# Values by head groups, row sums as GpSimd additions and six more VectorE steps in a mixed attention kernel

## The chip, the cores and the metric

The kernel runs on one core of a Trainium2 chip. The metric is the device time of one launch in microseconds, as the median of several runs. The core has TensorE (PE in the profile), VectorE (DVE), ScalarE (ACT), GpSimd (POOL) and SyncE (SP), which here only issues DMAs.

## The reference

There is one sequence of 2048 rows with 512 columns, in bf16, and 32 heads of 16 columns.

```python
g = sigmoid((x * gate_w).sum(-1, keepdims=True))
# branch A, linear attention: feature maps of q and k
pq = einsum("bhsd,hdf->bhsf", q, w_phi);  pk likewise from k
phi_q = concat([softmax(pq), softmax(-pq)]);  phi_k likewise
kv = einsum("bhsf,bhsd->bhfd", phi_k, v);  z = phi_k summed over s
a = (phi_q @ kv) / (phi_q @ z + 1e-6)  @ A_wo
# branch B, softmax attention on the same x with its own weights
p = softmax(q @ k.T * 16 ** -0.5);  b = (p @ v) @ B_wo
return g * a + (1 - g) * b
```

## The kernel before

Most of the work is branch B: 32 heads of 2048 x 2048 scores, each of which needs an exponential. The heads are handled in 32 *sets*, one for each of 4 chunks of 512 queries (`qc`), 4 groups of eight heads (`g`) and the two parities of heads in the group (`par`). A set goes over the 16 tiles of 128 keys (`kt`). Each `kt` gives two score tiles of 128 x 1024 in PSUM (`qk`, line 752), and two engines share the exponentials. For most `kt` ScalarE takes the exponential itself (line 771, two instructions). For the others, whose number for each set stands in `NDVE` (117 in all), VectorE builds the exponential from integer operations in a *step*: two reads of scores into 16-bit integers (line 761, `di`), then over 2048 elements a mask (line 777, `dm`), a product (line 780, `dw`) and a second mask (line 784, `de`). TensorE multiplies either result with the values (`pv`, lines 794 and 807); a VectorE step needs two such products of four matmuls, a ScalarE one needs one. The values lie in `vB`, with 16 columns and a column of ones for each head.

Around this stand *fills*: the projections of q, k and v (`q_proj`, `k_proj`, `v_proj`, all through line 475), branch A and the output projection (lines 891 and 899). Values are made two row tiles at a time for all heads at once, in a 1024-wide PSUM tile of the ring `R_r` that the scores use as well, and VectorE evacuates them (line 469, `vB`). All of that falls into the first two sets, whose entries in `NDVE` are 1 and 1.

Branch A makes 32 feature-map tiles (`phi`, 16 for keys and 16 for queries). Each has a fill, two exponentials on ScalarE (line 634) into one of four buffers of 1024 (`eA_r`, in the space of the weights `WAT`), row sums of 16 elements on VectorE (line 636), an addition of the sums into a check value on GpSimd (line 638), a reciprocal on VectorE (line 640) and the product on GpSimd (line 641).

Rows 0 to 511 of x are loaded plainly and turned on TensorE (line 550), with the two halves copied by ScalarE (line 553) and VectorE (line 554). The other three chunks of 512 rows come by transposing DMAs (line 409) on the SP queue.

The order on each engine isn't written by hand: `_Sched` lists the operations with priorities (in units `ut`, 32 to a set), assumed durations and dependencies, places them one after another, and writes the order of each engine with semaphore waits. It keeps GpSimd operations and the VectorE operations `dm`, `dw`, `de` and `qm` apart in its plan (`shared`, `port`); nothing enforces that at run time.

Of the kernel before, what the change touches and what calls it, by code (L numbers as in the profile page):

```python
# [6 lines left out]
BF16 = mybir.dt.bfloat16  # L7
# [3 lines left out]
ALU = mybir.AluOpType  # L11
# [22 lines left out]
VROW = H * VW + 16  # L34
NDVE = [1, 1, 4, 4, 4, 3, 4, 4, 3, 4, 3, 4, 4, 3, 5, 4, 4, 3, 4, 3, 5, 3, 4, 4, 5, 3, 4, 4, 4, 3, 5, 4]
# [11 lines left out]
STAY = 1.0  # L47
PAIRS = (0, 1, 2, 3, 4, 5, 6, 7)
RUSH = 1.5
HOLD = 0.4  # L50
WARM = 10
RUSH_K = 20.0
RUSH_O = 25.0
RUSH_1 = 8.0
QLEAD1 = 28
LATE_A = 0
VLEAD = 3.0
KLEAD1 = 24
KLEAD = 40
QLEAD = 32  # L60
EARLY = 8.0
# [268 lines left out]
def _build(ctx, nc, A_x, A_wqkv, A_w_phi, A_wo, B_wqkv, B_wo, gate_w, out):  # L330
# [19 lines left out]
    vB_ = sb([128, NT, VROW], name="vB")  # L350
    vB = vB_[:, :, 0:H * VW].rearrange("p t (h c) -> p t h c", c=VW)
    vA = sb([128, NT, 8, 66], name="vA")
# [22 lines left out]
    eA_r = _Slots([watv[:, 1024 * i:1024 * (i + 1)] for i in range(4)])  # L375
# [28 lines left out]
    xs = D_all[0].bitcast(BF16).rearrange("p (i c) -> p i c", c=D)  # L404
    op_x0 = dma("sp", -100, 3.6, xs, A_x[0, 0:NQ, :].rearrange("(i p) c -> p i c", p=128), name="x0")
    op_x = [None]
    for c in range(1, QC):
        op_x.append([add("sp", -100 + c, 2.5,
                         lambda e, c=c: e.dma_start_transpose(xT[:, :, NQ * c:NQ * (c + 1)], A_x[0, NQ * c:NQ * (c + 1), :]),  # L409
                         name=f"x{c}", dma=7.0)])  # L410
# [3 lines left out]
    op_wv = dma("act", -98, 6.0, W_Bv[:], wbv[:, :, 2 * D:3 * D], name="wv")  # L414
    op_wk1 = dma("act", -97, 8.0, W_Bk[:, :, 128:D], wbv[:, :, D + 128:2 * D], name="wk")
    op_wq1 = dma("act", -96, 8.0, W_Bq[:, :, 128:D], wbv[:, :, 128:D], name="wq")
    op_wat = add("sp", -90, 3.0, lambda e: e.dma_start_transpose(WAT[:], A_wqkv[:, 0:2 * D]), name="wat", dma=3.0)
# [22 lines left out]
    op_vpad = [pool(-99, 0.2, lambda e: e.memset(vB_[:, :, H * VW:VROW], 0.0), name="vpad")]  # L440
# [59 lines left out]
    def q_proj(g, c, prio, tile, off):  # L500
# [4 lines left out]
        if (g, c) == (0, 0):  # L505
# [3 lines left out]
            for j in range(4):  # L509
                ms.append(add("dve", prio + 0.01 * j, 0.39, lambda e, j=j: e.tensor_scalar(  # L510
                    qt.ap[:, j, :], q3(), masks[:, j:j + 1], None, op0=ALU.mult),
                    deps=[ev, op_masks] + (ms if j == 3 else []), tiles=[qt], name=f"qm{g}{c}{j}"))
            ev_q[g, c] = ms
# [11 lines left out]
    def v_proj(st, n, prio):  # L525

        tile = _Tile(M_r if n == 1 else R_r)
        fs = [fill(prio, tile, 512 * i, lambda t, i=i: xT[:, t, 128 * (st + i):128 * (st + i + 1)], lambda t: W_Bv[:, t, :],
                   op_x[st // 4] + [op_wv], f"vf{st}") for i in range(n)]
        use_wv.extend(fs)  # L530
        src = lambda: tile.ap[:, 0:512 * n].rearrange("p (t h d) -> p t h d", t=n, d=16)
        e1 = evac("dve", prio, lambda: vB[:, st:st + n, :, 0:16], src, fs, [tile], n=512 * n, name=f"vev{st}")
        for i in range(n):
            ev_v[st + i] = e1
# [7 lines left out]
    tx = _Tile(R_r)  # L542
    txv = lambda: tx.ap.bitcast(BF16).rearrange("p (t q) -> p t q", q=NQ)
    xtp = []
    for t in range(KT):

        def fn(e, t=t):
            ins = None
            for i in range(4):
                ins = e.transpose(txv()[:, t, 128 * i:128 * (i + 1)], xs[:, i, 128 * t:128 * (t + 1)], ident[:])  # L550
            return ins
        xtp.append(add("pe", -80 + t, 0.3, fn, deps=[op_x0, op_id], tiles=[tx], mode="full", name="xtp"))
    op_x[0] = [add("act", -80, 0.9, lambda e: e.copy(xT[:, 0:2, 0:NQ], txv()[:, 0:2, :]), deps=xtp[0:2], tiles=[tx], name="xev"),
               add("dve", -80, 0.6, lambda e: e.tensor_copy(xT[:, 2:4, 0:NQ], txv()[:, 2:4, :]), deps=xtp[2:4], tiles=[tx], name="xev")]
    I_r.tenant[0] = _Tile(None)
    I_r.tenant[0].ops = xtp
    tq = _Tile(R_r)
    k_proj(0, 0, -50, tq, 0, "act")
    q_proj(0, 0, -49, tq, 512)
    tk1 = _Tile(R_r)  # L560
# [4 lines left out]
    for st in range(0, NT, 2):  # L565
        if st // 2 in PAIRS:
            v_proj(st, 2, ut(2 * st) - VLEAD)
        else:
            v_proj(st, 1, ut(2 * st) + 0.5)
            v_proj(st + 1, 1, ut(2 * st + 2) + 0.5)  # L570


    for g in range(1, KT):
        base = 64 * g - (KLEAD1 if g == 1 else KLEAD)
        for c in range(QC):
            t = _Tile(M_r)
            k_proj(g, c, ut(base + 8 * c), t, 0)
        t = _Tile(M_r)
# [46 lines left out]
    def phi(prio, w, st, dst, dst_deps, dst_tiles):  # L625

        tile, ee, ss = _Tile(M_r), _Tile(eA_r), _Tile(ss_r)
        f = fill(prio, tile, 0, lambda t: xT[:, t, 128 * st:128 * (st + 1)], lambda t: Wp[:, w, t, :],
                 ev_wp[0] + ev_wp[1] + op_x[st // 4], f"pf{w}{st}")
        if w == 1:  # L630
# [5 lines left out]
        o6 = add("dve", prio + 5, 1.13, lambda e: e.tensor_reduce(  # L636
            ss.ap[:, 0, :], ee.ap.rearrange("p (g f) -> p g f", f=DH), AX.X, ALU.add), deps=o5, tiles=[ee, ss])
# [9 lines left out]
    for st in range(NT):  # L647
        prio = ut(100 + 16 * st)
# [9 lines left out]
    for lo, hi in ((0, 4), (4, 8)):  # L658
        tkv = _Tile(M_r)
        kvo = []  # L660
        for g in range(lo, hi):
# [6 lines left out]
            kvo.append(add("pe", ut(360 + 3 * g), 0.5, fn, deps=op_phk + ev_vA + kvo[-1:], tiles=[tkv], mode="full", name="kv"))  # L668
        kvw = lambda tkv=tkv: tkv.ap[:, 0:260].rearrange("p (g c) -> p g c", c=65)
        op_kz.append(add("dve", ut(384), 0.334, lambda e, kvw=kvw, lo=lo, hi=hi: e.tensor_tensor(  # L670
# [429 lines left out]
```

## Time and profile before

| quantity | value |
|---|---|
| median of 3 runs | 791.6 us (791.0 to 792.72) |
| profiled execution, its own time | 790.62 us |
| its span | 788.8 us |
| mean granted TensorE clock | 0.998 |
| ScalarE busy | 764.3 us, 97% |
| VectorE busy | 710.5 us, 90% |
| TensorE busy | 708.3 us, 90% |
| GpSimd busy | 121.1 us, 15% |

Busy is the time in which an engine had an instruction under way. Matmuls are pipelined and their ends are modelled, so TensorE's busy time includes waiting that overlaps the drain of the matmul in front.

### The profile page before, as it was taken

What the parts mean: (1) busy time and instruction counts of PE and PEld (TensorE: products, weight loads), DVE (VectorE), ACT (ScalarE), POOL (GpSimd) and SP (SyncE); (2) the same over time, 40 slices, a digit from 0 to 9 for tenths busy, and PEclk for the clock granted to TensorE, in tenths of its full rate; (3) what the DMA queues carried; (4) which work ended last, traced back from release to release, by engine and by line L of the source; (5) the groups of instructions that cost most, each with busy time, mean ns of one, the idle gap of its engine ahead of it and who ended that gap; (6) DMA issues with size and microseconds to landing.
All of it is one profiled execution on the core that took longest, in us unless ns stands there. A gap on an engine that the chain in (4) does not pass through costs nothing.

```text
span 788.8 us, 13621 instructions
## 1 busy us (share of the span) xinstructions
PE 708.3 (90%) x5645; PEld 224.7 (28%) x5716; DVE 710.5 (90%) x883; ACT 764.3 (97%) x865; POOL 121.1 (15%) x123
## 2 busy tenths in 40 slices
PE   8899999999999898998888999899998999988886
PEld 3223232222222222332222323222232232222222
DVE  2456999999999999999999999999999999999993
ACT  4989999999999999999999999999999999999995
POOL 7000002022233322111112010310111101120000
PEclk9999999999999999999999999999999999999999
DMA  9100000000000000023110121210111101120000
GB/s 240 28 8 2 11 4 1 10 6 1 14 1 8 9 1 14 1 68 41 28 21 21 30 19 34 48 23 19 27 22 40 35 14 27 35 42 1 7 1 30
DMA packets 55923, 19.57 MB, mean 25 GB/s; under 512 B 48304, under 2 KB 55856, under 8 KB 55856
## 3 DMA queue, kind: packets, MB, share of 16 engines
q1 hardware_dynamic: 52960, 17.06, 10.4%
q10 hardware_dynamic: 2640, 1.57, 0.7%
q8 instruction: 46, 0.75, 0.4%
q14 instruction: 21, 0.17, 0.1%
q0 software_dynamic: 256, 0.02, 0.0%
HBM read 3.69 MB, written 2.10 MB: 7 GB/s over the span
## 4 chain that ended last, share of the span: by engine, by line
ACT 87%; PE 6%; DVE 4%; DMA 2%; SPq 1%; issue 0%
ACT E L771 80%; ACT WAT L634 4%; PE ps L752 2%; ACT phiK L771 2%; PE ps L475 1%; DVE D L761 1%; DMA xT<-in_A_x_dram 1%; ACT vA L771 1%; PE ps L891 1%; PE ps L807 1%; SPq L521 1%; DVE D L777 1%; DVE D L780 1%; SPq L409 1%; PE ps L665 0%; DMA WB<-WB 0%
## 5 line engine op out<-in xcount | busy, mean ns | idle before, releaser
L771 ACT ACTIVATE E<-ps 128x1024 bf16<-128x1024 f32 x766 | 713.2, 1185 | 4.3 <-PE ps L807 2.2
L752 PE MATMUL ps<-q,kT 64*128 64x512 bf16 x2048 | 362.8, 385 | 58.1 <-ACT E L771 45.7
L761 DVE TENSOR_SCALAR D<-ps 128x1024 int16<-128x1024 f32 x234 | 284.5, 1216 | 21.7 <-PE ps L752 21.1
L752 PEld LDWEIGHTS ps<-q,kT 64*128 64x128 bf16 x2048 | 89.8, 93 | 275.2 <-ACT E L771 214.3
L807 PE MATMUL ps<-E,vB 128*32 128x512 bf16 x1532 | 149.1, 389 | 5.0 <-issue 4.3
L780 DVE TENSOR_TENSOR D<-D 128x2048 bf16<-128x2048 bf16 x117 | 141.4, 1209 | 0.6
L794 PE MATMUL ps<-D,vB 128*32 128x512 bf16 x936 | 90.8, 386 | 1.6 <-issue 1.0
L638 POOL TENSOR_TENSOR acc<-acc,ss 128x64 f32<-128x64 f32 x32 | 24.9, 778 | 435.4 <-DVE ss L636 435.4
L777 DVE TENSOR_SCALAR D<-D 128x2048 int16<-128x2048 int16 x117 | 83.8, 717 | 1.1
L784 DVE TENSOR_SCALAR D<-D 128x2048 int16<-128x2048 int16 x117 | 81.7, 698 | 0.1
L807 PEld LDWEIGHTS ps<-E,vB 128*32 128x32 bf16 x1532 | 37.8, 93 | 85.4 <-issue 77.5
L475 PE MATMUL ps<-xT,WB 128*128 128x512 bf16 x111 | 40.2, 388 | 3.3 <-ACT WAT L634 1.4
L634 ACT ACTIVATE WAT<-ps 128x512 bf16<-128x512 f32 x64 | 39.6, 755 | 0.0
L636 DVE TENSOR_REDUCE ss<-WAT 128x64 f32<-128x1024 bf16 x32 | 38.8, 1212 | 0.6 <-ACT WAT L634 0.4
L475 PE MATMUL ps<-Wp,xT 128*128 128x512 bf16 x98 | 38.0, 389 | 0.5 <-DVE OT L469 0.3
L641 POOL TENSOR_TENSOR phiK<-WAT,ss 128x1024 bf16<-128x1024 bf16 x16 | 35.6, 2222 | 10.7 <-DVE ss L640 10.7
L641 POOL TENSOR_TENSOR WB<-WAT,ss 128x1024 bf16<-128x1024 bf16 x16 | 33.5, 2096 | 14.3 <-DVE ss L640 14.3
L794 PEld LDWEIGHTS ps<-D,vB 128*32 128x32 bf16 x936 | 23.7, 94 | 37.5 <-issue 29.0
L469 DVE CAST vB<-ps 128x1024 bf16<-128x1024 f32 x8 | 9.8, 1225 | 22.0 <-PE ps L475 22.0
L835 PE MATMUL ps<-ident,OT 128*128 128x128 f32 x128 | 27.6, 300 | 0.5 <-ACT WAT L634 0.3
L891 PE MATMUL ps<-phiK 128*128 128x512 bf16 x74 | 25.8, 386 | 0.8 <-issue 0.3
L848 POOL TENSOR_TENSOR acc<-acc,rB 128x64 f32<-128x64 f32 x8 | 5.1, 633 | 133.9 <-DVE rB L840 133.9
(98 smaller groups left out, 351.2 us busy)
## 6 DMA issues: line engine op xcount, KB each, us to landing
out_dram<-Wp SPq DMA_DIRECT2D x16, 128.0 KB, 1.7
q<-qs SPq DMA_DIRECT2D x120, 16.0 KB, 1.8
WB<-in_B_wqkv_dram ACTq DMA_DIRECT2D x2, 384.0 KB, 8.6
D<-in_A_x_dram SPq DMA_DIRECT2D x1, 512.0 KB, 4.5
WB<-in_B_wqkv_dram ACTq DMA_DIRECT2D x1, 512.0 KB, 6.8
WAv<-in_A_wqkv_dram SPq DMA_DIRECT2D x1, 512.0 KB, 4.1
phiK<-in_A_wo_dram SPq DMA_DIRECT2D x1, 512.0 KB, 4.0
phiK<-in_B_wo_dram SPq DMA_DIRECT2D x1, 512.0 KB, 4.8
```

Source lines behind the costliest of these rows:

```text
L475: f = add("pe", prio - rush + 0.01 * t, MM, lambda e, t=t: e.matmul(tile.ap[:, off:off + 512], lhsT=lhs(t), rhs=rhs(t), start=(t == 0), st ...
L634: o5 = [add("act", prio + 1, 0.478, lambda e, a=a: e.activation(ev()[:, :, a, :], P(), ACTF.Exp, scale=1.0 - 2.0 * a), deps=[f], tiles=[ti ...
L636: o6 = add("dve", prio + 5, 1.13, lambda e: e.tensor_reduce(ss.ap[:, 0, :], ee.ap.rearrange("p (g f) -> p g f", f=DH), AX.X, ALU.add), dep ...
L641: return add("pool", prio + 7, 1.95, lambda e: e.tensor_tensor(dst().rearrange("p (g f) -> p g f", f=DH), ee.ap.rearrange("p (g f) -> p g ...
L752: ins = e.matmul(r.ap[:, 512 * i:512 * (i + 1)], lhsT=kT[p0:p0 + 64, g, 128 * kt:128 * (kt + 1)], rhs=qt.ap[p0:p0 + 64, 2 * pair + par, :] ...
L761: last_di = [add("dve", when - 6, 1.133, lambda e, r=r, I=I, part=part: e.tensor_scalar(I.ap[:, 1024 * part:1024 * (part + 1)], r.ap, EXP_ ...
L771: exps.append(add("act", when, 0.904, lambda e, r=r, E=E: e.activation(E.ap, r.ap, ACTF.Exp, scale=EXP_SCALE), deps=[q], tiles=[r, E], nam ...
L777: d1 = add("dve", pd, 0.06 + 0.54 * nk, lambda e, I=I, F=F, n=n: e.tensor_scalar(F.ap[:, 0:n], I.ap[:, 0:n], 0x007F, 0x3F00, op0=ALU.bitwi ...
L780: d4 = [add("dve", pd + 0.01 * y, 1.133, lambda e, I=I, F=F, lo=2048 * y: e.tensor_tensor(F.ap[:, lo:lo + 2048].bitcast(BF16), I.ap[:, lo: ...
L784: d2 = add("dve", pd + 0.1, 0.06 + 0.54 * nk, lambda e, I=I, n=n: e.tensor_scalar(I.ap[:, 0:n], I.ap[:, 0:n], -128, 0x0001, op0=ALU.bitwis ...
L794: ins = e.matmul(O.ap[32 * s:32 * s + 32, :], lhsT=vB_[:, kt, VW * h:VW * h + 32], rhs=w.ap.bitcast(BF16)[:, base + 1024 * (s % 2) + 512 * ...
L807: ins = e.matmul(O.ap[32 * s:32 * s + 32, :], lhsT=vB_[:, kt, VW * h:VW * h + 32], rhs=es[s % 2].ap[:, 512 * (s // 2):512 * (s // 2 + 1)], ...
```

## The change

It has four parts, and the order that `_Sched` writes is new throughout, since priorities and constants change with them.

- Values are made by group of eight heads: `v_proj(g, c)` makes four row tiles for one group as 16 matmuls of 128 columns in one 512-wide tile of `M_r`, and VectorE evacuates 512 columns. Only group 0 is due at the start; groups 1 to 3 come with the keys of their group. In `vB` the groups lie in reverse order (`vcol`), and the weights of group 0 are loaded on their own.
- Rows 512 to 1023 of x are loaded plainly as well and turned on TensorE (`turn(1)`).
- The row sums of the feature maps are four GpSimd additions that halve 1024 elements to 64; `eA_r` has two buffers, and one buffer `tr_r` holds partial sums.
- `NDVE` sums to 123 (sets 1 and 2: 3 and 4). The masks of the first q tile are waited for one by one.

```diff
-NDVE = [1, 1, 4, 4, 4, 3, 4, 4, 3, 4, 3, 4, 4, 3, 5, 4, 4, 3, 4, 3, 5, 3, 4, 4, 5, 3, 4, 4, 4, 3, 5, 4]
+NDVE = [3, 4, 4, 4, 3, 3, 4, 4, 4, 4, 4, 4, 4, 3, 3, 5, 5, 3, 4, 4, 4, 3, 5, 4, 4, 3, 4, 4, 5, 3, 5, 3]
...
-STAY = 1.0
-RUSH = 1.5
-HOLD = 0.4
+STAY = 3
+RUSH = 2.0
+HOLD = 0.3
...
-RUSH_O = 25.0
+RUSH_O = 10
...
+PK0 = 170
+PKS = 19
+PQ0 = 480
+PQS = 28
...
-    eA_r = _Slots([watv[:, 1024 * i:1024 * (i + 1)] for i in range(4)])
+    eA_r = _Slots([watv[:, 1024 * i:1024 * (i + 1)] for i in range(2)])
+    tr_r = _Slots([watv[:, 2048:3840].bitcast(F32).rearrange("p (a b) -> p a b", b=64)])
...
+    op_xs = [dma("sp", -100 + c, 4.0 + 4.3 * c, xs[c], A_x[0, NQ * c:NQ * (c + 1), :].rearrange("(i p) c -> p i c", p=128), name="x0")
+             for c in range(2)]
...
-    op_wv = dma("act", -98, 6.0, W_Bv[:], wbv[:, :, 2 * D:3 * D], name="wv")
+    op_wv0 = dma("act", -98, 5.0, W_Bv[:, :, 0:128], wbv[:, :, 2 * D:2 * D + 128], name="wv0")
...
+    op_wv1 = dma("act", -95, 10.0, W_Bv[:, :, 128:D], wbv[:, :, 2 * D + 128:3 * D], name="wv")
...
-    def v_proj(st, n, prio):
-        tile = _Tile(M_r if n == 1 else R_r)
...
+    def v_proj(g, c, prio):
+        tile = _Tile(M_r)
...
+                for t in range(KT):
+                    ins = e.matmul(tile.ap[:, 128 * i:128 * (i + 1)], lhsT=xT[:, t, 128 * (4 * c + i):128 * (4 * c + i + 1)],
+                                   rhs=W_Bv[:, t, 128 * g:128 * (g + 1)], start=(t == 0), stop=(t == KT - 1))
...
-        o6 = add("dve", prio + 5, 1.13, lambda e: e.tensor_reduce(
-            ss.ap[:, 0, :], ee.ap.rearrange("p (g f) -> p g f", f=DH), AX.X, ALU.add), deps=o5, tiles=[ee, ss])
+        o6 = None
+        for n, d in ((8, 1.12), (4, 0.71), (2, 0.5), (1, 0.4)):
+            o6 = add("pool", prio + 5, d, lambda e, n=n: e.tensor_tensor(
+                tr(n), tr(2 * n)[:, :, 0:n], tr(2 * n)[:, :, n:2 * n], ALU.add), deps=[o6] if o6 else o5, tiles=[ee, ss, tr_], name="ared")
...
-        prio = ut(100 + 16 * st)
+        prio = ut(PK0 + PKS * st)
...
-        prio = ut(400 + 32 * st)
+        prio = ut(PQ0 + PQS * st)
```

More of the change, by code (lines that the diff above doesn't have):

```diff
@@ L541, in _build, with turn, fn @@
             deps=[z0], tiles=[tw, tz], mode="full", name="warm")
[L542 to L556, printed above, removed]
+    def turn(c):
+        tx = _Tile(R_r)
+        txv = lambda: tx.ap.bitcast(BF16).rearrange("p (t q) -> p t q", q=NQ)
+        xtp = []
+        for t in range(KT):
+            def fn(e, t=t):
+                ins = None
+                for i in range(4):
+                    ins = e.transpose(txv()[:, t, 128 * i:128 * (i + 1)], xs[c][:, i, 128 * t:128 * (t + 1)], ident[:])
+                return ins
+            xtp.append(add("pe", -80 + t + 33.5 * c, 0.26, fn, deps=[op_xs[c], op_id], tiles=[tx], mode="full", name="xtp"))
+        sl = slice(NQ * c, NQ * (c + 1))
+        op_x[c] = [add("act", -80 + 34 * c, 0.9, lambda e: e.copy(xT[:, 0:2, sl], txv()[:, 0:2, :]), deps=xtp[0:2], tiles=[tx], name="xev"),
+                   add("dve", -80 + 34 * c, 0.6, lambda e: e.tensor_copy(xT[:, 2:4, sl], txv()[:, 2:4, :]), deps=xtp[2:4], tiles=[tx], name="xev")]
+        I_r.tenant[c] = _Tile(None)
+        I_r.tenant[c].ops = xtp
+    turn(0)
     tq = _Tile(R_r)
@@ L564, in _build @@
     k_proj(0, 3, -46, tk2, 0, "act")
[L565 to L570, printed above, removed]
+    for c in range(QC):
+        v_proj(0, c, ut(8 * c) - VLEAD)
     for g in range(1, KT):
@@ L885, in _build @@
         off = 512 if last and i == 1 else 0
-        prio = begin[i] if last else ut(545 + 128 * qc + 6 * i)
+        prio = begin[i] if last else ut(PQ0 + 145 + 4 * PQS * qc + 6 * i)
         sl, sb_ = slice(128 * st, 128 * (st + 1)), slice(128 * i, 128 * (i + 1))
```

90 lines of the change are left out of this document (50 added, 40 removed).

## The prediction

> **What bounds the kernel now.** I read the page's busy times and chain first, then the busy time by stretch, the chain in order of time, the groups by line with shapes apart, and last the timeline of VectorE and GpSimd side by side.
>
> ```profile
> span 788.8 us, 13621 instructions
> PE 708.3 (90%) x5645; PEld 224.7 (28%) x5716; DVE 710.5 (90%) x883; ACT 764.3 (97%) x865; POOL 121.1 (15%) x123
> ACT 87%; PE 6%; DVE 4%; DMA 2%; SPq 1%; issue 0%
> ```
> ScalarE carries the chain and is hardly idle. The time of this execution is 790.62 us, so 1.82 us lie around the span; it is 0.98 us under the median of 791.6. All sums below are against 790.62.
>
> I cut the span at the first exponential, at the end of the first two head sets (60 exponentials on ScalarE) and at its last exponential.
>
> ```profile
> core 0: us, PE busy (x) PEld busy (x) DVE busy (x) ACT busy (x) POOL busy (x), PEclk, DMA share, GB/s
> 0.00:11.55 11.55, 9.17 (x46) 3.89 (x47) 3.24 (x8) 2.89 (x3) 8.08 (x23) 1.00 0.91 243
> 11.55:74.00 62.45, 57.00 (x403) 18.02 (x407) 29.50 (x33) 57.23 (x64) 7.54 (x11) 1.00 0.20 42
> 74.00:777.40 703.40, 636.43 (x5167) 200.29 (x5227) 674.69 (x836) 701.84 (x796) 104.47 (x86) 1.00 0.09 19
> 777.40:788.80 11.40, 5.68 (x43) 2.51 (x36) 3.04 (x8) 2.33 (x4) 1.01 (x3) 0.88 0.17 52
> ```
> After 74 us ScalarE is idle for 703.40 - 701.84 = 1.6 us in all, and VectorE is busy for 95.9%: two full engines, with ScalarE ahead. Before 74 us it is otherwise. ScalarE has 62.45 - 57.23 = 5.2 us of gaps and VectorE is busy for 29.50 of 62.45. That is where the old step counts (1 and 1) leave room.
>
> ```profile
> 1.26 4.49 SPq L409
> 5.81 8.64 DMA xT<-in_A_x_dram
> 43.08 1.19 PE ps L475 x5
> 46.97 1.19 PE ps L475 x5
> 50.16 25.77 ACT E L771 x28
> 133.07 26.58 ACT E L771 x29
> ```
> This is the chain in order of time. Early it runs through the transposing load of x and, at 43 and 47 us, through projections on TensorE; from 50 us it is ScalarE's exponentials back to back, one each 26.58 / 29 = 0.917 us.
>
> **The change part by part.**
>
> *Steps.* The counts go from 117 to 123: sets 1 and 2 from 2 to 7, sets 3 to 32 from 115 to 116. A step moved takes two exponentials off ScalarE: 10 x 0.917 = 9.2 us early and 2 x 0.917 = 1.8 us late. On VectorE a step is two line 761, one 777, one 780 and one 784.
>
> ```profile
> L761 DVE TENSOR_SCALAR D<-ps 128x1024 int16<-128x1024 f32 x234 | 284.5, 1216 | 21.7 <-PE ps L752 21.1
> L780 DVE TENSOR_TENSOR D<-D 128x2048 bf16<-128x2048 bf16 x117 | 141.4, 1209 | 0.6
> L777 DVE TENSOR_SCALAR D<-D 128x2048 int16<-128x2048 int16 x117 | 83.8, 717 | 1.1
> L784 DVE TENSOR_SCALAR D<-D 128x2048 int16<-128x2048 int16 x117 | 81.7, 698 | 0.1
> L636 DVE TENSOR_REDUCE ss<-WAT 128x64 f32<-128x1024 bf16 x32 | 38.8, 1212 | 0.6 <-ACT WAT L634 0.4
> L469 DVE CAST vB<-ps 128x1024 bf16<-128x1024 f32 x8 | 9.8, 1225 | 22.0 <-PE ps L475 22.0
> L469 DVE COPY OT<-ps 128x512 f32<-128x512 f32 x31 | 21.0, 678 | 1.3 <-PE ps L807 1.0
> L641 POOL TENSOR_TENSOR phiK<-WAT,ss 128x1024 bf16<-128x1024 bf16 x16 | 35.6, 2222 | 10.7 <-DVE ss L640 10.7
> L852 POOL TENSOR_TENSOR acc<-acc,rB 128x64 f32<-128x64 f32 x8 | 2.6, 321 | 0.7
> ```
> A step costs (284.5 + 141.4 + 83.8 + 81.7) / 117 = 5.05 us of VectorE; that is a little high, since neighbouring instructions overlap. One more late step is +5.05, five more early ones +25.3.
>
> *Reduce to tree.* The 38.8 us of line 636 leave VectorE, all of them after 74 us. GpSimd gets per tile adds that write 512, 256, 128 and 64 elements. No row has these. Between line 852 (64 elements, 0.32) and the uncontended line 641 below (1024 elements, 1.93, bf16 with one operand broadcast) a straight line gives 0.21 us plus 1.68 ns per element: 1.07 + 0.64 + 0.43 + 0.32 = 2.46 us, 79 us for 32 tiles. GpSimd is busy for 121 us, so it goes to about 200 us, a quarter of the span. The bounds for one tile are 4 x 0.32 = 1.3 us and 4 x 1.93 = 7.7 us; I stay near the line because the ops span it. The Trainium skill, "GPSIMD Engine Reference", section "When to use GPSIMD", gives a reduction along the free dimension to VectorE and calls GpSimd about twice as slow on two-input operations; its 4497 ns for 2048 elements would make the tree about 2.1 us by an estimate, so by the rule as by the rows the sum takes longer on GpSimd than 1.21 us. The sum below is unchanged by it, because the time is taken from an engine with room.
>
> *What the tree costs VectorE.* GpSimd and VectorE hold each other up:
>
> ```profile
> 194.88 2.78 POOL L641 TENSOR_TENSOR phiK<-WAT,ss 128x1024 bf16<-128x1024 bf16 x1 [1.49 <-DVE ss L640]
> 196.93 1.28 DVE L784 TENSOR_SCALAR D<-D 128x2048 int16<-128x2048 int16 x1
> 198.14 0.68 DVE L777 TENSOR_SCALAR D<-D 128x2048 int16<-128x2048 int16 x1
> 229.13 1.93 POOL L641 TENSOR_TENSOR phiK<-WAT,ss 128x1024 bf16<-128x1024 bf16 x1 [0.36 <-DVE ss L640]
> ```
> Line 784 starts at 196.93 while line 641 runs to 194.88 + 2.78 = 197.66, and ends at 198.21, 0.55 us after it: it did nothing until GpSimd was through. How much of this there is now, from the groups for 120 to 700 us, and then for 700 to 777 us, where GpSimd hardly works:
>
> ```profile
> L777 DVE TENSOR_SCALAR D<-D 128x2048 int16<-128x2048 int16 x93 | 67.5, 726 | 0.8
> L784 DVE TENSOR_SCALAR D<-D 128x2048 int16<-128x2048 int16 x92 | 64.7, 703 | 0.0
> L784 DVE TENSOR_SCALAR D<-D 128x2048 int16<-128x2048 int16 x15 | 10.2, 682 | 0.0
> L777 DVE TENSOR_SCALAR D<-D 128x2048 int16<-128x2048 int16 x14 | 9.5, 676 | 0.1
> ```
> 93 x 0.050 + 92 x 0.021 = 6.6 us of stalls for 104.47 us of GpSimd work. The order written by the scheduler mostly keeps the two apart. In that proportion 79 us more cost 5 us; I take 7, since the adds follow ScalarE and not VectorE, so that their start is less tied to VectorE's own order. Were the starts random, 123 x 3 instructions would meet an add with a chance of 79 / 700, 42 times, and wait half of it, length weighted 0.37 us: 16 us. With everything serial it is 79 us. Behind the row stands the Trainium skill, "SBUF — State Buffer", section "SBUF: two separate sides": an exclusive lock on a shared port pair, held for the whole instruction, which also a VectorE operation with two SBUF inputs takes; for line 780 no row here shows that.
>
> VectorE after the first two sets is then 674.69 + 5.05 - 38.8 + 8 x 0.68 (values of two later groups) + 7 = 653.4 us of about 701.6: 93%, less full than now. ScalarE stays the bound there. Its gaps may grow from 1.6 to 2.4 us as stalls bunch: late stretch -1.8 + 0.8 = -1.0 us.
>
> *Slots.* The exponentials of the feature maps get two buffers for four, and one tree buffer. A third tile's exponentials on ScalarE would wait for the first tile's product on GpSimd, and the exponentials of the scores queue behind them.
>
> ```profile
> 123.73 0.98 ACT WAT L634 x2
> ...
> 318.38 0.98 ACT WAT L634 x2
> ```
> The 16 tiles of keys begin on average (318.38 - 123.73) / 15 = 13 us apart, and the new spacing is 19/16 of that, 15.4; the queries' goes from 32 units to 28. The GpSimd chain is 2.46 + 0.32 + 1.93 us and a reciprocal, some 6 us. Zero, then; if the cover went, each tile would hold ScalarE by at most that chain.
>
> *Values by groups.* 64 matmuls of 512 columns become 256 of 128, half of them now after the first two sets.
>
> ```profile
> 5.40 1.05 PE L550 MATMUL ps<-ident,D 128*128 128x128 bf16 x16
> 6.04 1.01 ACT L553 COPY xT<-ps 128x1024 bf16<-128x1024 bf16 x1 [0.54 <-PE ps L550]
> PEld ps L752 <- ACT E L771: 214.3, 600, 0.8
> ```
> At 1.05 / 16 = 0.066 us the early half costs 8.4 us where 64 x 0.238 (1.19 / 5 above) = 15.2 stood: TensorE gets 7 us back in the stretch in which it was the chain. Late it takes 8.4 us, hidden by the 214 us in which it waits for ScalarE. On VectorE 9.8 us of evacuation leave early and 8 x 0.68 = 5.4 come.
>
> *Second load of x.* ScalarE copies one more half block: +1.0 us. The plain load frees the SP queue from one transposition, so rows 1024 onward come sooner; a sixth load on ScalarE's queue lies ahead of the first copy. I count both at zero, with 1 us either way: the first exponential waits for the masks of q, not for either.
>
> *Early sum.* ScalarE's work is 57.23 - 9.2 + 1.0 = 49.0 us. VectorE's is 29.50 - 9.8 + 25.3 + 5.4 + 0.7 (its half of x) = 51.1, some 2 to 3 less with overlaps: both nearly full. So not all gaps vanish; I take 4.0 of the 5.2. The stretch is 53.0 for 62.45: -9.4 us (bounds -13, with no gaps, and -3, with VectorE at 85%).
>
> Sum: 790.62 - 9.4 - 1.0 = 780.2; head and tail unchanged. The median stood 0.98 above the profiled run, which gives 781.2.
>
> **The rivals.** *Forecast* (chance 0.68): ScalarE keeps the chain, 776 to 784.5 us. For it: 1.6 us of gaps in 703 while VectorE was at 95.9%, and VectorE is relieved.
>
> *The early steps don't pay* (0.12): set 1 and 2 become a wait of PV for VectorE. 51.1 us at a fill of 85% are 60 us, so the stretch gains 2 to 3 us for 9.4: 785 to 789.5. For it: before 74 us VectorE waited for TensorE, 22.0 us in front of the value evacuations alone. Against: the projections it waited for are what leaves.
>
> *The lock makes VectorE the bound* (0.16, slower). VectorE today fills 95.9% beside a full ScalarE; of 701.6 us that is 672.8, and without stalls from adds it needs 646.4. So 26.4 us of stalls are free, and each beyond costs about 1.04. The time is over 792.4 from 37.5 us on, nearly half of all adds' time. At 50 us it is 805, with everything serial 836. Against: today 6% of GpSimd's time returns as stalls. The Trainium skill's rule of engine selection, cited above, would favour this rival; the trace so far does not.
>
> *Nothing to be measured* (0.04): gains and stalls cancel, 790 to 793. A difference of 0.2%, 1.6 us, is about the least that a measurement of this kernel can tell.
>
> The likeliest gives 781.2. The range of 775 to 791 holds the forecast and the second case and leaves out the slower case and some of its neighbour. Faster is 0.68 + 0.12 = 0.80, same 0.04, slower 0.16.
>
> **What would show it.** Right: no reduce on VectorE; twelve fewer exponentials in the groups of line 771; the 50th exponential ends near 63 us; ScalarE idle under 3 us from there to its last; an add of 512 at about 1.07 us; lines 777 and 784 at 0.70 to 0.76 on average. Wrong: ScalarE waiting for scores under a VectorE that is above 97% busy, means of 777 and 784 above 0.85, or exponentials of the feature maps waiting for GpSimd.

## The result, and the profile after

The changed kernel takes 787.84 us (median of 6 runs, 786.9 to 789.1) against 791.58 us before. The ratio is 0.9951 with a 95% interval of 0.9937 to 0.9965: faster by 3.7 us, where 10.4 were forecast. The time lies inside the stated range of 775 to 791, but the gain is about a third of the forecast one. The profiled execution took 787.98 us.

The head of the page after, and the busy time in the same four stretches as before: up to the first exponential, to the end of the first two sets (now 50 exponentials), to ScalarE's last exponential, and the tail.

```profile
span 786.2 us, 14251 instructions
PE 731.3 (93%) x5948; PEld 237.2 (30%) x5948; DVE 720.7 (92%) x890; ACT 756.2 (96%) x854; POOL 218.8 (28%) x251
ACT 64%; PE 21%; DVE 12%; issue 1%; SPq 1%; DMA 1%
core 0: us, PE busy (x) PEld busy (x) DVE busy (x) ACT busy (x) POOL busy (x), PEclk, DMA share, GB/s
0.00:14.80 14.80, 11.20 (x67) 5.52 (x68) 3.75 (x9) 3.80 (x5) 8.06 (x23) 0.88 0.99 231
14.80:64.30 49.50, 47.40 (x418) 17.95 (x416) 42.69 (x50) 47.71 (x55) 9.19 (x11) 1.00 0.18 41
64.30:775.50 711.20, 667.28 (x5439) 211.41 (x5435) 671.23 (x825) 702.33 (x794) 200.59 (x214) 1.00 0.09 19
775.50:786.20 10.70, 5.45 (x31) 2.29 (x31) 3.04 (x8) 2.33 (x4) 1.00 (x3) 0.90 0.17 54
```

The first two sets end at 64.3 us for 74.0: the early gain of 9.7 us is there. The third stretch holds two exponentials fewer and yet lasts 711.2 us for 703.4, so 7.8 us of the gain are lost here. ScalarE, which held 87% of the chain, holds 64%, and VectorE and TensorE have come into it, though VectorE is busy for only 671.23 of 711.20 us, 94.4%, less than the 95.9% of before.

The groups of VectorE's product (line 806) and masks (803 and 810), the four GpSimd additions (662) and the feature-map exponentials on ScalarE (656). GpSimd's own product of a feature-map tile is line 667 now and was line 641.

```profile
L806 DVE TENSOR_TENSOR D<-D 128x2048 bf16<-128x2048 bf16 x123 | 150.4, 1224 | 1.0
L803 DVE TENSOR_SCALAR D<-D 128x2048 int16<-128x2048 int16 x123 | 96.6, 786 | 1.2
L810 DVE TENSOR_SCALAR D<-D 128x2048 int16<-128x2048 int16 x123 | 90.0, 732 | 0.2
L662 POOL TENSOR_TENSOR WAT<-WAT 128x512 f32<-128x512 bf16 x32 | 42.0, 1312 | 256.8 <-ACT WAT L656 256.7
L662 POOL TENSOR_TENSOR WAT<-WAT 128x256 f32<-128x256 f32 x32 | 31.4, 981 | 2.4
L662 POOL TENSOR_TENSOR WAT<-WAT 128x128 f32<-128x128 f32 x32 | 19.3, 603 | 2.4
L662 POOL TENSOR_TENSOR ss<-WAT 128x64 f32<-128x64 f32 x32 | 12.4, 388 | 2.5
L656 ACT ACTIVATE WAT<-ps 128x512 bf16<-128x512 f32 x64 | 39.1, 739 | 0.1
```

Lines 803 and 810 were lines 777 and 784 before, at 717 and 698 ns. Summed over the trace after the first two sets, and counting what an instruction took over 0.69 us (masks) or 1.23 us (product) where that is more than 0.1 us, VectorE stalls for 20.0 us in 37 instructions; before it was 6.5 us in 11. By the GpSimd instruction that runs beside them, 11.7 of the 20.0 us lie beside the additions (short ones into check values included), in 29 instructions, and 8.3 us beside GpSimd's product, in 8. Before, all 6.5 us lay beside the product.

One burst shows how a stall reaches ScalarE. It is the timeline of VectorE, then of GpSimd, of TensorE and of ScalarE:

```profile
311.84 0.69 DVE L803 TENSOR_SCALAR D<-D 128x2048 int16<-128x2048 int16 x1
312.44 1.64 DVE L810 TENSOR_SCALAR D<-D 128x2048 int16<-128x2048 int16 x1
314.01 1.75 DVE L806 TENSOR_TENSOR D<-D 128x2048 bf16<-128x2048 bf16 x1
315.68 1.21 DVE L787 TENSOR_SCALAR D<-ps 128x1024 int16<-128x1024 f32 x1
...
311.84 4.17 POOL L662 TENSOR_TENSOR WAT<-WAT 128x512 f32<-128x512 bf16 x3 [4.57 <-ACT WAT L656]
316.09 0.29 POOL L662 TENSOR_TENSOR ss<-WAT 128x64 f32<-128x64 f32 x1
...
316.95 0.60 PE L778 MATMUL ps<-q,kT 64*128 64x512 bf16 x4 [0.74 <-DVE D L787]
...
314.34 2.02 ACT L797 ACTIVATE E<-ps 128x1024 bf16<-128x1024 f32 x2
317.38 1.02 ACT L797 ACTIVATE E<-ps 128x1024 bf16<-128x1024 f32 x1 [1.03 <-PE ps L778]
```

The additions begin when ScalarE's exponentials end, not when VectorE has room. Line 810 takes 1.64 us for 0.69, line 806 right behind it 1.75 for 1.23; line 787, which frees a score tile, starts some 1.5 us late. TensorE waits for it with the next scores (line 778), and ScalarE stands idle for 1.03 us. That VectorE's product, with two inputs in SBUF, is held up as well is what the Trainium skill says in "SBUF — State Buffer", section "SBUF: two separate sides"; the 1.75 us agree.

GpSimd's product does the same, and more:

```profile
257.87 2.25 POOL L667 TENSOR_TENSOR phiK<-WAT,ss 128x1024 bf16<-128x1024 bf16 x1 [2.32 <-DVE ss L666]
258.26 2.41 DVE L803 TENSOR_SCALAR D<-D 128x2048 int16<-128x2048 int16 x1
...
263.58 7.44 ACT L797 ACTIVATE E<-ps 128x1024 bf16<-128x1024 f32 x8 [1.29 <-PE ps L778]
```

It starts 0.39 us ahead of line 803, which then takes 2.41 us for 0.69, and ScalarE pauses for 1.29 us. Of ScalarE's pauses over 0.15 us in the third stretch, five end within 6.5 us of the start of such a stall, 4.7 us in all: three of them (1.29, 0.72 and 0.92 us) behind a stall of 1.72 or 1.73 us beside the product, and two (1.03 and 0.72) behind a burst of 0.95 and 0.52 us beside the additions. No other stall has a pause right behind it but a further 1.0 us in three short ones, while TensorE has half its clock (last section). A pause of 1.41 us at 628 us lies behind the load of a query tile, and two pauses at 94 and 116 us, 0.7 us together, stand in the kernel with short additions and product (below) as well.

### The profile page after: what moved, and what is told of

It reads as the page before. It is cut to its first block, busy times and chain, and to the rows that moved or that the text cites. A ratio compares the mean times of both kernels' runs of the same rounds, so it can differ in the third digit from the quotient of the medians.

```text
span 786.2 us, 14251 instructions
## 1 busy us (share of the span) xinstructions
PE 731.3 (93%) x5948; PEld 237.2 (30%) x5948; DVE 720.7 (92%) x890; ACT 756.2 (96%) x854; POOL 218.8 (28%) x251
## 4 chain that ended last, share of the span: by engine, by line
ACT 64%; PE 21%; DVE 12%; issue 1%; SPq 1%; DMA 1%
ACT E L797 59%; PE ps L778 8%; DVE D L787 4%; PE ps L487 3%; PE ps L833 3%; ACT WAT L656 2%; DVE D L803 2%; DVE D L806 2%; PE ps L917 2%; ACT phiK L797 2%; PE ps L820 2%; DVE D L810 1%; SPq L533 1%; ACT vA L797 1%; PE ps L547 1%
## 5 line engine op out<-in xcount | busy, mean ns | idle before, releaser
L797 ACT ACTIVATE E<-ps 128x1024 bf16<-128x1024 f32 x754 | 703.4, 1144 | 8.7 <-PE ps L778 7.6
L787 DVE TENSOR_SCALAR D<-ps 128x1024 int16<-128x1024 f32 x246 | 298.5, 1213 | 29.4 <-PE ps L778 28.4
L662 POOL TENSOR_TENSOR WAT<-WAT 128x512 f32<-128x512 bf16 (+2 forms) x96 | 92.7, 965 | 261.6 <-ACT WAT L656 256.7
L806 DVE TENSOR_TENSOR D<-D 128x2048 bf16<-128x2048 bf16 x123 | 150.4, 1224 | 1.0
L803 DVE TENSOR_SCALAR D<-D 128x2048 int16<-128x2048 int16 x123 | 96.6, 786 | 1.2
L810 DVE TENSOR_SCALAR D<-D 128x2048 int16<-128x2048 int16 x123 | 90.0, 732 | 0.2
L487 PE MATMUL ps<-xT,WB 128*128 128x512 bf16 x128 | 49.1, 402 | 2.8 <-issue 2.2
L487 PE MATMUL ps<-Wp,xT 128*128 128x512 bf16 x128 | 49.2, 391 | 2.3 <-DVE oB L867 1.8
L917 PE MATMUL ps<-phiK 128*128 128x512 bf16 x88 | 31.4, 387 | 0.6 <-ACT WAT L656 0.6
L487 PE MATMUL ps<-WAv,xT 128*128 128x512 bf16 x64 | 23.5, 388 | 1.7 <-ACT WAT L656 1.6
L481 DVE COPY OT<-ps 128x512 f32<-128x512 f32 x31 | 21.1, 680 | 2.0 <-PE ps L833 1.0
## 6 DMA issues: line engine op xcount, KB each, us to landing
WB<-in_B_wqkv_dram ACTq DMA_DIRECT2D x3, 384.0 KB, 10.3
```

What stands on the lines that cost most here:

```text
L487: f = add("pe", prio - rush + 0.01 * t, MM, lambda e, t=t: e.matmul(tile.ap[:, off:off + 512], lhsT=lhs(t), rhs=rhs(t), start=(t == 0), st ...
L662: o6 = add("pool", prio + 5, d, lambda e, n=n: e.tensor_tensor(tr(n), tr(2 * n)[:, :, 0:n], tr(2 * n)[:, :, n:2 * n], ALU.add), deps=[o6] ...
L787: last_di = [add("dve", when - 6, 1.133, lambda e, r=r, I=I, part=part: e.tensor_scalar(I.ap[:, 1024 * part:1024 * (part + 1)], r.ap, EXP_ ...
L797: exps.append(add("act", when, 0.904, lambda e, r=r, E=E: e.activation(E.ap, r.ap, ACTF.Exp, scale=EXP_SCALE), deps=[q], tiles=[r, E], nam ...
L803: d1 = add("dve", pd, 0.06 + 0.54 * nk, lambda e, I=I, F=F, n=n: e.tensor_scalar(F.ap[:, 0:n], I.ap[:, 0:n], 0x007F, 0x3F00, op0=ALU.bitwi ...
L806: d4 = [add("dve", pd + 0.01 * y, 1.133, lambda e, I=I, F=F, lo=2048 * y: e.tensor_tensor(F.ap[:, lo:lo + 2048].bitcast(BF16), I.ap[:, lo: ...
```

## The experiments

Before was measured anew beside each group of experiments: 791.58 us beside the changed kernel, 792.33 beside the next four kernels, 790.86 beside the four after them and 791.58 beside the last three. Kernels of different groups are therefore best compared by their ratios to before.

**Short additions, and short additions with a short product.** The order of every engine is that of the changed kernel; the additions, then also GpSimd's product, work on 64 elements and leave out the rest.

```diff
-                tr(n), tr(2 * n)[:, :, 0:n], tr(2 * n)[:, :, n:2 * n], ALU.add)
+                row n of tr_ (or ss), 64 elements, from two rows of 64, ALU.add)
...
-            dst()[all 64 groups of 16] = ee * reciprocals
+            dst()[groups 0 to 3] = ee * reciprocals
```

> The changed kernel with the same order on every engine; the four GpSimd additions of a feature-map tile remain, but each works on 64 elements (two of the sixteen terms are summed and doubled three times). Theory (the adds hold the port that VectorE's lines 803, 806 and 810 need, in bursts that reach ScalarE): GpSimd falls by about 65 us, the means of 803 and 810 fall from 0.79 and 0.73 to about 0.72, ScalarE's gaps after the first two sets fall by 4 to 6 us, time 782 to 784 against 788. Rival (the new order and its fill density make the gaps, not the adds): gaps unchanged, 787 to 789.

> As the kernel with short adds, same order, and the GpSimd product of each feature-map tile also works on 64 of its 1024 elements. Theory of the port: the rest of the late gaps that are not a late query load or a clock drop goes too, means of 803 and 810 at 0.68, time 779 to 781. Rival (order): 786 to 789. If the product and not the adds is what hurts, this one gains and the short adds alone do not.

Measured: 784.44 us (ratio to before 0.9892, 0.986 to 0.9925) and 779.88 us (0.9833, 0.9803 to 0.9863). The stretch after the first two sets, and the masks, of the second kernel:

```profile
64.50:767.50 703.00, 647.29 (x5371) 210.81 (x5435) 654.97 (x825) 700.43 (x794) 99.12 (x214) 1.00 0.09 19
L807 DVE TENSOR_SCALAR D<-D 128x2048 int16<-128x2048 int16 x123 | 86.3, 703 | 1.2
L814 DVE TENSOR_SCALAR D<-D 128x2048 int16<-128x2048 int16 x123 | 84.0, 683 | 0.2
```

The order is the same and GpSimd is busy for half as long, with 1.1 us of stalls left: the stretch takes 703.00 us for 711.20, where the forecast had 703.4 - 1.0 = 702.4. One pause of 1.19 us is left in it, in which TensorE waits for a query tile's load. So the new order alone is not at fault. What GpSimd's work does to VectorE costs the changed kernel 787.84 - 779.88 = 8.0 us, or 0.9951 - 0.9833 = 1.2%, 9.3 us, by the ratios: 3.4 us (4.7 by the ratios) with the additions, 4.6 more with the product. The split is rough: with short additions alone the four runs took 783.08 to 787.05 us, and the profile, of the slowest of them, shows gaps of 7.7 us for 8.9, not the 4 to 6 us less that were expected. Its masks have means of 0.744 and 0.694, and its stalls are 9.1 us, of which 8.1 lie beside the product.

**The tree alone.** The kernel before with the four additions, two buffers and the partial-sum buffer, nothing else but the order that `_Sched` then writes.

```diff
-        o6 = add("dve", prio + 5, 1.13, lambda e: e.tensor_reduce(
+        for n, d in ((8, 1.12), (4, 0.71), (2, 0.5), (1, 0.4)):
+            o6 = add("pool", prio + 5, d, ...
```

> The kernel before with one part of the change: the row sums as four GpSimd additions, two buffers for the exponentials and one for partial sums; steps, values, loads and constants as before. My forecast's view (VectorE's relief is worth nothing by itself, stalls stay hidden): 790 to 792, no difference. Theory of the port in bursts: ScalarE's gaps grow by 5 to 8 us, 796 to 799. Rival (order of the rest of the change is to blame): 790 to 792 too, and the loss must then show in the kernel without the tree.

Measured: 799.04 us, ratio 1.0086 (1.0056 to 1.0116). The 38.8 us of the reduction are gone from VectorE, and the kernel is 7 us slower:

```profile
PE 711.8 (89%) x5648; PEld 226.9 (28%) x5716; DVE 695.1 (87%) x851; ACT 766.1 (96%) x865; POOL 223.2 (28%) x251
L782 DVE TENSOR_SCALAR D<-D 128x2048 int16<-128x2048 int16 x117 | 92.9, 796 | 1.1
L785 DVE TENSOR_TENSOR D<-D 128x2048 bf16<-128x2048 bf16 x117 | 145.6, 1245 | 1.0
```

VectorE is at 87%, and the masks of line 782 are at 796 ns for 717; stalls by the same count are 21.3 us, of which 11.5 or a little more lie beside the product and the rest beside the additions. A VectorE with room doesn't protect ScalarE.

**Without the tree.** First the changed kernel with row sums on VectorE, the step counts of before from set 3 on and the feature-map spacing of before.

```diff
-PK0, PKS, PQ0, PQS = 170, 19, 480, 28;  NDVE sums to 123
+PK0, PKS, PQ0, PQS = 100, 16, 400, 32;  NDVE sums to 122
```

> The changed kernel without the tree: row sums on VectorE, four buffers, the step counts of before from set 3 on (3, 4 and then 115, together 122), and the feature-map spacing of before; values by groups and the second plain load stay. Theory (early part works, the loss comes with the tree): early gain of 10 us kept, one less late step costs 1.8, late gaps of 2 to 4 us as VectorE is at 97%: 781 to 784. Rival (VectorE too full without the tree): late gaps of 8 us or more, 787 or slower.

Measured: 808.67 us, ratio 1.0206 (1.0175 to 1.0237). Expected were 781 to 784, and the run tells nothing on the question: ScalarE has three pauses of 12, 6 and 5 us between 157 and 198 us, the longest here, and the scheduler's own order for this kernel holds them.

```profile
151.90 5.89 ACT L792 ACTIVATE E<-ps 128x1024 bf16<-128x1024 f32 x6
169.54 2.10 ACT L792 ACTIVATE E<-ps 128x1024 bf16<-128x1024 f32 x2 [11.74 <-PE ps L773]
```

Then with other spacing and counts (3 and 5, then 114), so that the order has no pause as long as these:

> The changed kernel with the row sums on VectorE again and four buffers; 122 steps (3 and 5 in the first two sets, then 114), keys' feature maps 16 units apart from 170, queries' 32 from 430, chosen so that the order has no long pause of ScalarE of its own, which the earlier kernel without the tree had. Theory (the tree relieves VectorE of about as much as the port takes back): the same as the changed kernel, 786 to 790. Rival A (the tree is a net loss): 780 to 784. Rival B (the tree is worth much, VectorE is too full without it): 794 or more.

Measured: 795.45 us, ratio 1.0051 (1.0028 to 1.0074), with runs from 791.89 to 799.96; the median is in the second rival's reach of 794 or more. The stretch from the 50th exponential on:

```profile
63.50:782.00 718.50, 671.27 (x5413) 211.29 (x5410) 680.62 (x851) 703.18 (x795) 102.83 (x86) 0.99 0.09 19
```

With 3 and 5 steps the first two sets hold 48 exponentials here, which end at 61.6 us; the 50th ends at 63.5, about as early as with the tree. So the early gain needs no tree. But the late stretch is 718.50 us for 711.20. VectorE's work there is 680.62 us, the reduction among it, and ScalarE stands idle for 718.50 - 703.18 = 15.3 us. The kernel is 795.45 - 787.84 = 7.6 us slower than the changed one, with one step fewer in all. That this is the tree's worth is not shown: stalls are 2.6 us here, and of ScalarE's longest pauses only one, of 3.09 us to 72.1 us, has TensorE waiting for VectorE, for a copy; those of 3.59 and 1.79 us, with 1.03 behind, come when TensorE waits for DMAs (2.95 us for a query tile up to 298.4 us, 1.69 us for a turned feature map up to 431.8 us). The order and the spacing of the feature maps differ as well.

**The kernel before with a short product.** If the stalls of before were hidden, taking them away gives nothing.

```diff
-            dst()[all 64 groups of 16] = ee * reciprocals
+            dst()[groups 0 to 3] = ee * reciprocals
```

> The kernel before in its own order, with the GpSimd product of a feature-map tile on 64 of its 1024 elements. My forecast's reading (the 6.6 us of stalls of before are hidden by VectorE's slack): 790 to 792, no gain. Theory (each stall of VectorE reaches ScalarE in part even there): 787 to 789, half the stalls back.

Measured: 790.14 us, ratio 0.999 (0.998 to 0.9999).

```profile
L777 DVE TENSOR_SCALAR D<-D 128x2048 int16<-128x2048 int16 x117 | 79.8, 683 | 1.1
L784 DVE TENSOR_SCALAR D<-D 128x2048 int16<-128x2048 int16 x117 | 78.9, 674 | 0.1
```

The masks are at 0.683 and 0.674 us, about what the prediction took as free (0.676 and 0.682), the stalls are gone, and the kernel gains a tenth of a per cent, 0.8 us. Nearly all of the stalls of before were hidden. What the 6.5 us cost before is 1.6 us at most, by the interval.

**Weights ahead of the second load of x.** Order and work of the changed kernel; two weight loads go from ScalarE's queue to SP's, between the two plain loads of x. This tests the later first exponential of the profile after (14.80 us for 11.55).

```diff
+    for n, o in enumerate((op_wk0, op_wq0)):
+        sch.order["act"].remove(o)
+        o.eng = "sp"
+        sch.order["sp"].insert(1 + n, o)
```

> The changed kernel, every engine's order kept, but the loads of the first weights of keys and queries go out on the SP queue between the two plain loads of x, instead of on ScalarE's queue beside them. Theory (the second plain load delays those weights, and TensorE's clock drops in the wait): first projection near 7.3 us for 8.9, no half clock at 9 us, first exponential at 11.5 to 12.5 for 14.8, time 784 to 786. Rival (start is hidden, since ScalarE waits later for VectorE's steps): 787 to 789.

Measured: 787.61 us, ratio 0.996 (0.9945 to 0.9975): no difference to the changed kernel that could be told (0.2 us less by the medians, 0.7 more by the ratios), as the rival had it. In its profile the first exponential is at 13.74 us, the 50th ends 1.1 us earlier and the last 0.8 us. The start was not what was missing. A single profile's start also proves little: the short-product kernel above loads and starts just as before does and has its first exponential at 15.43 us, not 11.55.

**The product in four pieces.** Everything of the changed kernel is done; the product of 1024 elements is four instructions of 256, so that VectorE could get in between.

```diff
-            dst()[64 groups] = ee * reciprocals
+            for h in range(4):
+                dst()[groups 16h to 16h + 15] = ee * reciprocals
```

> The changed kernel in its order, with GpSimd's product of a feature-map tile in four pieces of 256 elements, one behind the other, semaphore on the last. Theory (VectorE waits for the rest of one GpSimd instruction, so shorter instructions mean shorter waits): means of 803 and 810 fall by 0.03 to 0.05, 784 to 787. Rival (a GpSimd instruction waiting in its queue takes the port again at once, so VectorE waits for all four): unchanged or slower, 788 to 791.

Measured: 786.08 us, ratio 0.9934 (0.9911 to 0.9956).

```profile
L808 DVE TENSOR_SCALAR D<-D 128x2048 int16<-128x2048 int16 x123 | 94.6, 769 | 1.2
L815 DVE TENSOR_SCALAR D<-D 128x2048 int16<-128x2048 int16 x123 | 90.0, 732 | 0.2
```

The masks were at 786 and 732, so little changes; the sum of stalls is 20.5 us for 20.0. But those that last over 0.8 us fall from 7 to 4, ScalarE's pauses right behind stalls fall from 4.7 to 3.0 us, and 1.8 us come back (1.3 by the ratios). That long stalls cost more than the same time in short ones would explain it, but the intervals of the two ratios overlap, so this is weak.

**GpSimd held to the plan.** The scheduler plans times for all operations; on the chip the order on each engine is fixed, but GpSimd starts as soon as its inputs are there. Here each GpSimd operation after 60 us of the plan, the product as well as the additions, also waits for the last VectorE mask or product that the plan starts ahead of it. No work is left out and no order changed.

```diff
+    k, held = 0, [d for d in sch.order["dve"] if d.shared]
+    for o in sch.order["pool"]:
+        while k < len(held) and held[k].start < o.start:
+            k += 1
+        if o.start > 60 and k and o.dma is None:
+            o.deps.append(held[k - 1])
```

> The changed kernel, order of every engine kept and nothing left out; each GpSimd operation after 60 us of the plan also waits for the last of VectorE's mask and product instructions that the plan puts ahead of it. In the changed kernel's trace 20 us of stalls of VectorE lie in 37 instructions, and behind nearly all of them stands a GpSimd operation that the plan has after the VectorE instruction, but that came first because VectorE was later than planned. Theory (it is this overtaking, not the sharing itself, that costs): stalls over 0.1 us fall from 20 to 5 us or less, time 780 to 783. Rival (sharing costs what it costs; a held GpSimd operation only delays the feature maps): 786 to 790.

Measured: 780.81 us, ratio 0.9858 (0.9836 to 0.988).

```profile
64.20:768.50 704.30, 666.10 (x5440) 210.68 (x5436) 662.93 (x825) 700.57 (x793) 163.55 (x214) 1.00 0.09 19
L803 DVE TENSOR_SCALAR D<-D 128x2048 int16<-128x2048 int16 x123 | 86.0, 700 | 1.2
L810 DVE TENSOR_SCALAR D<-D 128x2048 int16<-128x2048 int16 x123 | 89.5, 727 | 0.2
L662 POOL TENSOR_TENSOR WAT<-WAT 128x512 f32<-128x512 bf16 x32 | 37.9, 1184 | 256.9 <-DVE D L806 105.7 <-ACT WAT L656 76.8 <-DVE D L787 38.8
L662 POOL TENSOR_TENSOR WAT<-WAT 128x256 f32<-128x256 f32 x32 | 23.3, 728 | 22.0 <-DVE D L803 11.7 <-DVE D L810 5.9 <-DVE D L806 3.5
L662 POOL TENSOR_TENSOR WAT<-WAT 128x128 f32<-128x128 f32 x32 | 13.3, 415 | 11.2 <-DVE D L803 6.5 <-DVE D L810 1.9 <-DVE D L806 1.2
L662 POOL TENSOR_TENSOR ss<-WAT 128x64 f32<-128x64 f32 x32 | 9.9, 309 | 18.4 <-DVE D L806 12.4 <-DVE D L803 3.3 <-DVE D L810 1.0
```

The additions now wait mostly for VectorE (lines 806, 787, 803 and 810), and the kernel is faster for it, as GpSimd has room. Of the 8.0 us that GpSimd's work took, 7.0 are back (7.4 of 9.3 by the ratios; the interval overlaps with that of the short additions and product). Stalls halve, to 10.3 us in 25 instructions; that is over the 5 expected, and those over 0.8 us fall from 7 to 3. "Nearly all" was said too strongly: of the 26 stalls over 0.2 us in the changed kernel, 16, with 12.9 of 18.5 us, have a GpSimd operation beside them that the plan puts behind the VectorE instruction. Three of the 16 are GpSimd's product, with the stalls of 1.72 and 1.73 us, and all five stalls or bursts with a pause of ScalarE behind them are among the 16. That agrees with about half of the stalls gone. In the held kernel no pause of ScalarE over 0.15 us comes within 8 us behind a stall.

**The same waits on the tree alone.** They hold all of GpSimd's operations, as above.

```diff
+    (the six lines above, in the kernel with the tree alone)
```

> The kernel before with the tree alone, and the same extra waits of GpSimd. Theory (overtaking costs the 7 us of the kernel with the tree alone): 790 to 793, as before, since ScalarE is the bound. Rival: 797 to 800 as without the waits.

Measured: 791.96 us, ratio 1.0002 (0.9987 to 1.0017). The 7 us that the tree cost alone are gone. The order of every engine is that of the kernel with the tree alone.

```profile
74.10:777.00 702.90, 653.69 (x5225) 202.41 (x5225) 649.66 (x804) 701.72 (x796) 167.73 (x214) 1.00 0.09 19
L782 DVE TENSOR_SCALAR D<-D 128x2048 int16<-128x2048 int16 x117 | 82.2, 705 | 1.1
```

VectorE has 649.66 us of work where before had 674.69, and the late stretch is 702.90 for 703.40. ScalarE sets it; relief of VectorE by itself is worth nothing here. Stalls are still 10.8 us, in 21 instructions, and cost nothing that can be told.

**All that helped, together.** The held GpSimd operations, the weights first, and a query load that the plan reckons with 5.0 us for 3.0, because ScalarE has a pause in the changed kernel behind such a load (1.41 us, to 629.5 us). The last edit makes a new plan.

```diff
+    (the six lines above, and the four of the weights)
-    ... name=f"qsp{g}{c}", dma=3.0, parts=8)
+    ... name=f"qsp{g}{c}", dma=5.0, parts=8)
```

> As the changed kernel with the extra waits, and two small repairs: the first weights of keys and queries load on the SP queue between the two plain loads of x, and the load that spreads a query tile is planned at 5 us of latency for 3, so that the order is a new one, with the pause of 1.75 us at 629 us expected to go. Expected 777 to 781; if the pause was luck of the order and another one takes its place, 780 to 783 as with the waits alone.

Measured: 778.35 us, ratio 0.9833 (0.9815 to 0.9852): 13.2 us under before and 9.5 under the changed kernel. The pause behind the query load is gone. Between this and the held kernel lie 2.5 us, which were not divided between the two further edits and the new plan.

```profile
L803 DVE TENSOR_SCALAR D<-D 128x2048 int16<-128x2048 int16 x123 | 85.3, 694 | 1.2
```

## Why the prediction was right or wrong, point by point

**The early part was right.** Forecast was a gain of 9.4 us up to the end of the first two sets; the profiled executions show 74.0 - 64.3 = 9.7. Inside it two things missed in opposite ways: the stretch itself is 49.5 us for the 53.0 of the sum, with VectorE at 42.69 us of work and not some 48 to 51, and ScalarE's work at 47.71 us for 49.0, its gaps at 49.50 - 47.71 = 1.8 us where 4.0 had been left (53.0 - 49.0); against that stood a first exponential 3.25 us later in this profile. So the agreement of 9.4 and 9.7 is partly luck. VectorE's work was less in part because eight more reads of scores and four more products fall into the stretch, four steps and not the five counted. The head was taken as unchanged; part of its 3.25 us is the first projection, which starts at 8.94 us for 7.24 and meets half the clock (0.88 in the first row for 1.00). The second load may be the cause in part: with the weights ahead of it the first exponential came 1.1 us sooner, in one profile.

**The tree's price on GpSimd was nearly right.** A straight line between 64 and 1024 elements gave 2.46 us per tile. With GpSimd held to the plan the four take 1.184 + 0.728 + 0.415 + 0.309 = 2.64. The changed kernel shows 1.312 + 0.981 + 0.603 + 0.388 = 3.28, so VectorE holds GpSimd up as well.

**Slots, tail and the late values cost nothing that shows**, as counted: ScalarE is idle for 0.1 us ahead of the 64 exponentials of line 656, the tail is no longer than before (10.70 us for 11.40), and with short additions and product the late stretch, values in it, is within 0.6 us of the forecast.

**The step that failed is "What the tree costs VectorE"**, and what hung on it, ScalarE's gaps. The sum counted 7 us of new stalls, gaps of 2.4 us and a late stretch shorter by 1.0. Measured were 13.5 us more stalls (6.5 to 20.0), gaps of 711.20 - 702.33 = 8.9 us and a late stretch longer by 7.8. Of the 8.8 us missed there, 6.5 are gaps; the other 2.3 are ScalarE's own busy time, 702.33 us where 701.84 - 1.8 = 700.0 were counted. With short additions and product it is 700.43, so it goes with the pauses; why was not taken apart. In the group of ScalarE's exponentials from 75 to 765 us, before and after, the releaser is named:

```profile
L771 ACT ACTIVATE E<-ps 128x1024 bf16<-128x1024 f32 x717 | 667.9, 1186 | 1.5 <-PE ps L752 1.2 <-PE ps L807 0.2
L797 ACT ACTIVATE E<-ps 128x1024 bf16<-128x1024 f32 x706 | 658.9, 1142 | 8.6 <-PE ps L778 7.6 <-PE ps L833 0.4
```

Before it waited 1.2 us for scores, now 7.6, of which 1.4 are the query tile's load. Two arguments in that step were wrong.

First, the proportion. 6.6 us of stalls for 104 us of GpSimd work was taken over to the additions. But that work was mostly the product, which waits for VectorE's own reciprocal. Before, 10 of its 11 stalls have the product in the plan ahead of the VectorE instruction, and no pause of ScalarE over 0.15 us comes within 8 us behind them; only the one stall of 1.73 us came by overtaking, and a pause of 0.67 us follows it. The additions start when ScalarE has ended its exponentials. The prediction saw that and raised 5 to 7; measured are 11.7 us beside the additions. The estimate for random starts, 16 us, stood beside it and was about as far off on the other side. What the prediction did not count at all is that the product of the feature maps, whose stalls were hidden before, would overtake masks in the new order: its stalls went from 6.5 to 8.3 us only, but three of them now last 1.72 us or more with a pause behind them, and shortening the product was worth 4.6 us. With GpSimd held to the plan, additions and product together leave 10.3 us, 3.8 more than before.

Second, room. 93% of VectorE's time was taken as proof that 7 us of stalls, or up to 26, could be borne. Measured fill is 94.4%, lower than before, and VectorE never became the bound. A fill is an average: a burst such as the one at 312 us delays the release of a score tile at once, and ScalarE pauses before VectorE has had time to use its room. How much of a stall reaches ScalarE depends on its length and place: the 20.0 us of the changed kernel cost 8.0 to 9.3 us (against short additions and product, whose stalls are 1.1 us), while the 10.3 us with GpSimd held cost 0.9 to 2.0 and the 6.5 us of before 1.6 at most. The tree alone shows it most plainly: at a fill of 87% overall the kernel lost 7 us, and gained them back when only the starts of GpSimd's operations changed.

**The rivals.** The lock that makes VectorE the bound had GpSimd's hold on VectorE right, but the wrong way from it to a loss: its 37.5 us were never reached, and 20 us cost 8 to 9 with VectorE below full. "The early steps don't pay" named 785 to 789.5, which holds the measured time, for a reason that fell: the early steps paid in full. That the loss comes from when GpSimd meets VectorE is shown by 779.88 us with short additions and product and 780.81 with all work done and GpSimd held, where the forecast was 781.2. That these come so near to the forecast is luck in part: the sum charged 0.8 us for 7 us of stalls, and its head came out 3 us longer, its early stretch 3.5 us shorter.

**Which engine for the reduction.** That a reduction along the free dimension goes to VectorE (the Trainium skill, "GPSIMD Engine Reference", section "When to use GPSIMD") spoke against this change. The runs don't decide it: the tree takes 2.64 us on GpSimd for 1.21 on VectorE; added to the kernel before it cost 7 us, or nothing with GpSimd held; and the changed kernel at 787.84 us stands against 795.45 without the tree, in another order. That GpSimd and VectorE shut each other out for whole instructions (the Trainium skill, "SBUF — State Buffer", section "SBUF: two separate sides") agrees with the runs: line 803 ends 0.55 us behind the end of line 667 in the timeline at 258 us, 260.67 for 260.12.

**What stays open.** The 10.3 us of stalls that remain with GpSimd held lie beside the product (5.9 us) and the additions (4.4); why the plan still lets them meet was not taken apart. The sums of stalls do not order the kernels: with short additions alone 9.1 us of stalls in one profile go with a loss of 4.6 us (784.44 for 779.88, in runs that spread widely), with GpSimd held 10.3 us with one of 0.9 to 2.0, with the tree alone and GpSimd held 10.8 us with none. The pauses fit better: those with short additions alone come behind three stalls of 1.72 or 1.73 us, and in the two held kernels, whose longest stalls are 1.38 and 1.40 us, no pause follows a long stall. How long a stall a score tile can bear was not measured singly. What a tree on GpSimd is worth against the reduction on VectorE, in the changed kernel and with nothing else altered, was not measured either. Nor is it known how much of the gain of 1.8 us from the split product is more than the spread of the runs.

## What to carry to other kernels

A busy share below 100% is not room for stalls: ask how long one burst may be before the next engine's buffer runs dry, and count the bursts. When work moves to an engine that holds up a nearly full one, ask what starts it, and what starts the work that is there already; if it can overtake the full engine's planned instructions, tie its start to their order by an extra wait on the engine that has room. And when an order is made by a planner, look for pauses in the new plan before a difference between two kernels is put down to the edit.

## What the runs showed of the hardware

Line 806, a product of two bf16 operands in SBUF, is held up by GpSimd too: 1.75 us for 1.23 behind an addition. What comes first holds the other: line 803 takes 2.41 us for 0.69 behind line 667, and the addition of 64 elements takes 1.28 us for 0.29 when it starts at 253.87 us, behind line 806 of 253.79 to 255.00 us. So the order of arrival decides, not the amount of work: the same GpSimd work cost 8.0 to 9.3 us, or 0.9 to 2.0.

The first exponential came between 11.55 and 15.43 us in the profiles of the four kernels that start as before does. And in the profile after, TensorE stood idle for 1.68 us up to 335.10 us, behind the stall of 1.73 us at 332.0, and had half its clock from about 336.9 to 340.3 us, which shows as 0.93 between 336 and 360 us:

```profile
336.00:360.00 24.00, 23.17 (x152) 6.32 (x151) 18.59 (x23) 23.00 (x28) 13.69 (x15) 0.93 0.03 6
```

ScalarE paused for 0.72 us right behind the stall, and for 0.38, 0.22 and 0.40 us while the clock was low. So a stall can go on costing after its first pause. This happened once between the start and the tail in that profile, and it did not follow from the length of the wait alone: TensorE waited longer, 2.26 us, for the query tile up to 628.12 us, and kept its full clock.
